# First chunk of a recurrent attention and expert kernel: transposed x made directly by matmuls, values loaded as fp32 and cast, state copied, a new order

## The chip, the cores and the metric

The kernel runs on one core of a Trainium2 chip. The metric is the device time of one execution in microseconds (us). A profiled execution gives a span from its first to its last instruction, which is shorter than the device time.

## The reference, cut to what matters

Two stages follow each other. The first is a gated recurrence over 768 steps for 4 batches and 8 heads of width 48; the second a mixture of 4 dense experts, each applied to every row.

```python
f = 1 / (1 + exp(-f_logit))
for t in range(768):
    state = f[:, :, t, :, None] * state + einsum('bhd,bhe->bhde', k[:, :, t], v[:, :, t])
    y[:, :, t] = einsum('bhd,bhde->bhe', q[:, :, t], state)
x = y.transpose(0, 2, 1, 3).reshape(3072, 384)
p = domain_probs / (domain_probs.sum(-1, keepdims=True) + 1e-9)
out = sum(p[:, e:e+1] * (relu(x @ w1[e]) @ w2[e]) for e in range(4))     # w1 384x1024, w2 1024x384
```

## The kernel before

**Tiling.** The sequence is cut into 6 chunks of 128 steps; in each chunk all 4 batches are worked on, so a chunk gives 512 rows of x. Inside a chunk the recurrence is turned into matmuls: cumulative sums of log gates (`cs`, `cq`), their exponentials (`exps`, `expq`), products of these with q and k (`q`, `k`), transposes of the products (`tpq`, `tpk`, evicted by `ev_tp`), scores (`at`, evicted through a causal mask by `ev_at0` and `ev_at1`; two of these go through ScalarE and a mask on GpSimd, `mask1`), and `y` = scores times values. Chunks behind the first add a product with the carried state. After `y`, `kv` makes the state's new part, `ev_kv` adds it to `Sf`, and GpSimd scales and casts it (`sf`).

**From y to the experts.** The experts need x transposed. In the first chunk, `ev_y` evicts y as bf16, `xt` transposes it by three TensorE transposes and `ev_xt` evicts that to the tile xT. Then the expert matmuls: `h` (w1 times xT, a unit being twelve 128-wide matmuls in chunk 0 and three 512-wide ones afterwards), `relu`, `o` (times w2). From the second half of chunk 1 on, other forms of these run (`hs` and `p`).

**Loads.** SyncE (SP) issues the loads of f, k and q, one per batch in chunk 0 (197 KB each; f and q in packets of 384 bytes, k in packets of 192). GpSimd (POOL) issues transfers that also cast: the values v of chunk 0 as bf16 (`vb`, line 284), and all weights (line 303), in eleven pieces w0 to w10: w0 and w1 are the two halves of expert 0's w1, w2 and w3 those of expert 1's w1, w4 and w5 those of expert 0's w2, w6 to w10 whole matrices. w0 to w3 are written in packets of 1,024 bytes (384 packets a piece), w4 and w5 in packets of 768 (512 a piece). POOL works in order, and also does elementwise work; a load that it issues may be held back by `GATE` until another transfer has landed. Before, POOL's order is v0, v1, v2, w0, v3, then w1 and so on. In later chunks v is loaded by SP as fp32 and cast by an engine. The last piece, w10, is issued when chunk 1's first k load has landed.

**Order.** Nothing is reordered at run time: each engine works through its own list. The list comes from a small planner (`Plan.run`, line 92): each step (`Op`) has a cost per engine, dependencies, buffers that it takes and frees, and a priority. The planner walks forward in time, and whenever an engine is free it starts the ready step with the smallest priority. Priorities are due times plus corrections from the table `MOVES`. All transfers share one planned engine, "DMA", which carries one transfer after the other. Where PE is planned to have a longer hole ahead of the first expert matmul, filler matmuls (line 1022) are put in.

Of the kernel before, what the change touches and what calls it, by code (L numbers as in the profile page):

```python
# [8 lines left out]
FP32 = mybir.dt.float32  # L9
# [5 lines left out]
MOVES = (  # L15
# [24 lines left out]
class Op:  # L40


    def __init__(self, name, costs, emit, prio, deps=(), takes=(), frees=(), lag=0.0):
        self.name, self.costs, self.emit, self.prio = name, costs, emit, prio
        self.deps = [d for d in deps if d is not None]
        self.takes, self.frees, self.lag = list(takes), list(frees), lag
        if name.split(" ")[-1].startswith("0.") and {"ACT", "DVE"} & set(costs):
            self.lag += 0.1
        self.end = self.start = self.engine = None
        self.pad = 0  # L50
        self.port, self.turn = False, None


class Plan:


    LATENCY = 0.2

    def __init__(self, rooms):
        self.moves = dict(m.split("=") for m in MOVES.split(";") if m)  # L60
# [3 lines left out]
    def add(self, *args, **kw):  # L64
        op = Op(*args, **kw)
        by, _, engine = self.moves.get(op.name, "0").partition("@")
        op.prio += float(by)
        if engine:
            op.costs = {engine: op.costs[engine]}
# [67 lines left out]
def kernel(  # L137
# [23 lines left out]
    NT = B * T  # L161
    N2 = NT // 2
# [18 lines left out]
    P.slot[SPARE] = P.rooms["ps_m"].pop()  # L181

# [35 lines left out]
    nc.vector.memset(Sf, 0.0)  # L218
# [14 lines left out]
    for nm, a in (("f", f_logit), ("q", q), ("k", k), ("v", v)):  # L233
# [12 lines left out]
        "mp": ([128, 512], FP32),  # L246
    }

    alias = {"xT": "x", "xs": "x", "hs": "h", "ys": "yb", "praw": "o"}
    inbank = ("hp", "op", "pp", "mp")  # L250

    def tl(kind, *key):
# [10 lines left out]
        return tiles[kind, key]  # L263

# [62 lines left out]
    def gate2(c, b, n):  # L327
        g = tl("gp", c, b // 2).rearrange("t b h d -> t (b h) d")
        if c == 0:
            nc.scalar.activation(out=g[:, hh(b), 0:D].rearrange("t (j h) d -> t h j d", j=2),  # L330
# [740 lines left out]
```

## Time and profile before

| what | value |
|---|---|
| device time, median of 3 runs (lowest, highest) | 288.47 us (287.62, 289.21) |
| profiled execution, span | 285.7 us |
| median less span | 2.8 us |
| TensorE (PE) busy | 277.4 us |
| first expert matmul (`h`, line 489) | 18.18 us |
| last instruction on a compute engine (DVE, line 607) begins | 282.41 us |
| mean granted TensorE clock | 1.000 |

The profiled execution has its own span; what lies around it is not in the profile, so the difference to the median of the runs is kept as it is. A row of a timeline reads: start in us, length in us, engine, line, operation, what is written, what is read, shape, count, and in brackets the idle time before and what ended it. PEld is TensorE's weight load. A row of a DMA view reads: queue, packets, MB, and the time that the packets took as a share of 16 engines; packets overlap, so that share can be over 100%. Rows of the view by stretches give the stretch, its length, then the busy time of each engine with its number of instructions, the granted clock, the DMA share and GB/s.

### The profile page before, as it was taken

Reading aid. Unit: us, or ns where it says so; the run is one execution under the profiler, and the core shown is the slowest. Engines: PE = TensorE matmul, PEld = TensorE weight load, DVE = VectorE, ACT = ScalarE, POOL = GpSimd, SP = SyncE. Lnnn points to the kernel's source line nnn. Section 1 sums busy time; section 2 is a strip of 40 time slices with the busy share of each in tenths; the row PEclk is TensorE's granted clock in tenths of the full one; section 3 lists DMA queues with packets and bytes.
Section 4 is the critical chain, followed back from the end, with each engine's and each line's share of the span. In section 5 each row is a group of like instructions: output and inputs, shape, how many; then the busy total and the mean of one; then the engine's idle time right before and its main releaser. Section 6 shows DMA issues by size and latency. Waiting matters only on the chain.

```text
span 285.7 us, 7476 instructions
## 1 busy us (share of the span) xinstructions
PE 277.4 (97%) x3016; PEld 236.7 (83%) x3020; DVE 196.1 (69%) x402; ACT 180.6 (63%) x336; POOL 114.1 (40%) x186
## 2 busy tenths in 40 slices
PE   6889999999999999999999999999999999999995
PEld 4667555657877999999999998999899998999994
DVE  5794144697779896875888848886888730874374
ACT  6768756568657963586668766658638348836710
POOL 5999101528663760866036756343750000000000
PEclk9999999999999999999999999999999999999999
DMA  6999999999977999999879999989675210050003
GB/s 157 214 199 207 208 192 205 178 202 178 183 142 151 160 197 155 210 184 185 178 150 189 164 224 210 144 191 158 74 164 107 57 55 2 19 122 31 2 0 110
DMA packets 153687, 41.85 MB, mean 146 GB/s; under 512 B 144029, under 2 KB 152861, under 8 KB 153653
## 3 DMA queue, kind: packets, MB, share of 16 engines
q1 hardware_dynamic: 142404, 34.66, 65.0%
q0 software_dynamic: 11248, 6.72, 16.3%
q8 instruction: 23, 0.38, 0.6%
q14 instruction: 12, 0.09, 0.1%
HBM read 31.51 MB, written 4.72 MB: 127 GB/s over the span
## 4 chain that ended last, share of the span: by engine, by line
PE 78%; DMA 14%; POOL 5%; SPq 1%; issue 0%; DVE 0%; POOLq 0%
PE ps_m L521 33%; PE ps_m L580 29%; DMA w_sb<-in_moe_w_dram 10%; PE ps_m L504 6%; PE ps_m L489 4%; DMA k<-in_k_dram 4%; POOL w_sb L303 2%; PE ps_m L428 2%; PE ps_m L455 1%; POOL vb L284 1%; PE ps_m L451 1%; PE ps_m L338 1%; PE ps_m L461 1%; POOL AT L432 1%; SPq L290 1%
## 5 line engine op out<-in xcount | busy, mean ns | idle before, releaser
L521 PE MATMUL ps_m<-x,w_sb 128*128 128x256 bf16 x864 | 104.8, 273 | 0.0
L529 ACT ACTIVATE h<-ps_m 128x512 bf16<-128x512 f32 x111 | 66.2, 598 | 46.1 <-PE ps_m L521 38.8
L521 PEld LDWEIGHTS <-w_sb 128*128 128x128 bf16 x864 | 82.9, 98 | 9.4
L580 PEld LDWEIGHTS <-S 128*128 128x128 bf16 x576 | 48.7, 98 | 0.9
L607 DVE TENSOR_TENSOR o<-ps_m,o 128x192 f32<-128x192 f32 x91 | 31.3, 354 | 22.0 <-PE ps_m L580 21.0
L580 PEld LDWEIGHTS <-h 128*128 128x128 bf16 x432 | 36.2, 98 | 0.6
L504 PE MATMUL ps_m<-w_sb,h 128*128 128x384 bf16 x192 | 35.3, 326 | 0.4 <-DMA w_sb<-in_moe_w_dram 0.4
L489 PE MATMUL ps_m<-x,w_sb 128*128 128x128 bf16 (+2 forms) x260 | 34.5, 281 | 0.6 <-DMA w_sb<-in_moe_w_dram 0.4
L411 ACT ACTIVATE yb<-ps_m,pn 128x384 bf16<-128x384 f32 x54 | 28.1, 584 | 7.7 <-PE ps_m L455 6.4
L476 POOL TENSOR_TENSOR Sf<-Sf,egs 48x192 f32<-48x192 f32 x40 | 21.0, 526 | 27.1 <-DVE Sf L468 17.4
L444 DVE TENSOR_TENSOR AT<-ps_m,mask 128x512 bf16<-128x512 f32 x40 | 25.2, 683 | 8.6 <-PE ps_m L428 8.5
L500 ACT ACTIVATE h<-ps_m 128x512 bf16<-128x512 f32 (+1 forms) x42 | 22.5, 536 | 12.8 <-PE ps_m L489 11.8
L489 PEld LDWEIGHTS <-w_sb 128*128 128x128 bf16 x264 | 21.7, 98 | 9.5 <-DMA w_sb<-in_moe_w_dram 0.6
L544 DVE TENSOR_TENSOR S<-h 128x1024 bf16<-128x1024 bf16 x36 | 25.2, 713 | 6.1 <-ACT h L529 5.5
L580 PE MATMUL ps_m<-ts_sb,S 128*128 128x192 bf16 x288 | 29.2, 246 | 0.0
L580 PE MATMUL ps_m<-w_sb,S 128*128 128x192 bf16 x288 | 28.7, 246 | 0.0
L504 PEld LDWEIGHTS <-h 128*128 128x128 bf16 x192 | 18.3, 98 | 12.5 <-DMA w_sb<-in_moe_w_dram 0.9
L388 POOL TENSOR_TENSOR qk<-q,e 128x384 bf16<-128x384 f32 x19 | 22.7, 1205 | 14.5 <-ACT e L371 9.7
L580 PE MATMUL ps_m<-w_sb,h 128*128 128x192 bf16 x288 | 28.0, 246 | 0.0
L527 DVE TENSOR_SCALAR h<-ps_m 128x512 bf16<-128x512 f32 x33 | 22.4, 691 | 8.1 <-PE ps_m L521 7.5
L371 ACT ACTIVATE e<-ps_m 128x384 f32<-128x384 f32 x40 | 23.4, 704 | 5.8 <-PE ps_m L338 5.4
L388 POOL TENSOR_TENSOR qk<-k,e 128x384 bf16<-128x384 f32 x20 | 20.2, 1016 | 16.7 <-PE ps_m L580 7.4
(87 smaller groups left out, 317.5 us busy)
## 6 DMA issues: line engine op xcount, KB each, us to landing
out_dram<-o SPq DMA_DIRECT2D x23, 192.0 KB, 2.3
w_sb<-in_moe_w_dram POOLq DMA_DIRECT2D x5, 768.0 KB, 16.3
k<-in_k_dram SPq DMA_DIRECT2D x10, 384.0 KB, 5.6
q<-in_q_dram SPq DMA_DIRECT2D x10, 384.0 KB, 5.2
v<-in_v_dram SPq DMA_DIRECT2D x10, 384.0 KB, 5.4
f<-in_f_logit_dram SPq DMA_DIRECT2D x9, 384.0 KB, 4.6
w_sb<-in_moe_w_dram POOLq DMA_DIRECT2D x6, 384.0 KB, 8.6
f<-in_f_logit_dram SPq DMA_DIRECT2D x6, 192.0 KB, 3.7
```

What stands on the lines that cost most here:

```text
L371: nc.scalar.activation(out=o, in_=i, func=AF.Exp, scale=1.0 if j else -1.0)
L388: return engines[eng].tensor_tensor(out=tl("qk", c, b)[:, j, :, 0:D].rearrange("t (i r) d -> t i r d", r=2), in0=tl("qk"[j], c, b // 2)[:, ...
L411: nc.scalar.activation(out=ys, in_=y, func=AF.Copy, scale=pe)
L444: nc.vector.tensor_tensor(out=tl("AT", c, b)[:, r].rearrange("s i t -> s (i t)"), in0=tl("A", c, b, r).rearrange("s i t -> s (i t)"), in1= ...
L489: nc.tensor.matmul(out=hp(c, e, fc, n0, n1, nf)[:, f], lhsT=w1_sb[:, e, kk, (fc + f) * 128:(fc + f + 1) * 128], rhs=tl("xT", c)[:, kk, n0: ...
L500: nc.scalar.activation(out=dst, in_=src, func=AF.Relu)
L504: nc.tensor.matmul(out=tl("op", c, e, nt)[:, 0:Din], lhsT=tl("h", c, e, half_of(c, nt * T))[:, fc, nt * T:(nt + 1) * T], rhs=w2_sb[:, e, f ...
L521: nc.tensor.matmul(out=out_[:, f], lhsT=w1_sb[:, e, kk, (fc + f) * 128:(fc + f + 1) * 128], rhs=tl("xs", c, hf, p)[:, el, kk, :], start=(k ...
L529: nc.scalar.activation(out=dst, in_=tl("hp", c, hf, p, el, fc), func=AF.Relu)
L544: return nc.vector.tensor_tensor(out=o, in0=in0, in1=in1, op=op)
L580: nc.tensor.matmul(out=out_, lhsT=lhs[:, f, :], rhs=rhs[:, f, :], start=(first and el == 0 and f == 0), stop=(el == 1 and f == KH - 1), sk ...
L607: nc.vector.tensor_tensor(out=o, in0=src, in1=o, op=ALU.add)
```

## The change

1. **Transposed x directly (`pe_yt`, `yt`).** For all four batches of chunk 0, the values stand in a zero-padded tile `vp` (128 zeros, then for each head 48 values and 128 zeros). A 128-column window of that tile is the stationary operand and the scores of one head the moving one, so that the result is already x transposed: ten 128-wide matmuls per batch into one PSUM tile `yT`, evicted once to xT (`ev_xt`; in two parts for the last batch). `y`, `ev_y` and `xt` of chunk 0 go.
2. **Values as fp32.** v of chunk 0 is loaded by SP, as in later chunks, and cast into `vp` by an engine (`cast_v`): batch 1's on VectorE, batch 2's on ScalarE, batch 0's on POOL, batch 3's on VectorE. POOL's four loads of v go.
3. **State copied.** In chunk 0 `ev_kv` copies into `Sf` instead of adding (on ScalarE for three batches, on VectorE for one), and Sf's memset goes; four memsets of `vp` (128x768 words each) come.
4. **A new order.** `MOVES` gives way to `RANKS`, a whole list of priorities, one for each step; planned costs and delays are set anew; `GATE` now holds w0 until batch 0's f has landed and w1 until batch 1's v has landed.

What the built program then does in chunk 0, engine by engine (numbers are batches):

- SP: f2, f1, q2, k2, q1, f0, k1, f3, v1, q3, q0, k0, the probabilities, k3, v2, v0, v3 (before: f0, f1, k2, f2, k1, k0, q0, q1, q2, f3, k3, q3, the probabilities).
- POOL: product k2, w0, product q1, w1, w2, product q0, mask of batch 2, w3, mask of batch 1, w4, w5, cast of v0, w6, and on with states and weights.
- DVE: product q2, product k1, QK of batch 2, cast of v1, scores of 2, QK of 1, product k0, product q3, product k3, QK of 0, scores of 1 and 0.
- ACT: gates and exponentials, scores of batches 2 and 1, cast of v2, two copies of QK of batch 3, eviction of x of batch 2, state copies, then relu.
- PE: the chunk's matmuls, `yt` of batch 2, scores of 0, `kv` of 2, scores of 3, the first `h` (batch 2, w0), `yt` and `kv` of 1, `yt` and `kv` of 0, `h` of batch 1 with w1 and w0, `h` of batch 0 with w1, `yt` of 3, and on. Six filler matmuls stand in place of ten.

The core of the diff:

```diff
-    LATENCY = 0.2
+    LATENCY = 0.14
...
+    for c, b in DIRECT:
+        nc.vector.memset(tl("vp", c, b), 0.0)
...
     def load(c, nm, b, n):
-        if (c, nm) == (0, "v"):
-            ins[c, nm, b] = nc.gpsimd.dma_start(out=tl("vb", c, b), in_=srcs[nm][c, :, b * H:(b + n) * H, :])
-            if f"v{b}" in GATE:
-                after(ins[c, nm, b], ins[GATE[f"v{b}"]])
-            return
...
+    def v_pad(b):
+        return tl("vp", 0, b)[:, T:].rearrange("t (h x) -> t h x", x=VP)[:, :, 0:D]
+
     def cast_v(c, b, eng):
-        return copy(eng, tl("vb", c, b), tl("v", c, b // 2)[:, hh(b), :])
+        return copy(eng, v_pad(b) if (c, b) in DIRECT else tl("vb", c, b), tl("v", c, b // 2)[:, hh(b), :])
+
+    def pe_yt(b):
+        for kk in range(KD):
+            heads = [h for h in range(H) if h * D < (kk + 1) * 128 and (h + 1) * D > kk * 128]
+            for h in heads:
+                w0 = T + h * VP - (h * D - kk * 128)
+                nc.tensor.matmul(out=tl("yT", 0, b)[:, kk, :], lhsT=tl("vp", 0, b)[:, w0:w0 + 128], rhs=tl("AT", 0, b)[:, h % 2, h // 2, :],
+                                 start=(h == heads[0]), stop=(h == heads[-1]))
...
+            if c == 0:
+                copy(eng, Sf[rows, b], KV[rows, :, r, :])
+            else:
+                nc.vector.tensor_tensor(out=Sf[rows, b], in0=Sf[rows, b], in1=KV[rows, :, r, :], op=ALU.add)
...
-ORDER = "f0 k0 q0 f1 k1 q1 f2 f3 k2 q2 k3 q3"
-SEQ = "v0 v1 v2 w0 v3 w1"
+ORDER = "f0 k0 q0 f1 k1 q1 v0 f2 k2 q2 v1 f3 k3 q3 v2 v3"
...
-GATE = {"v0": (0, "k", 1), "v1": (0, "k", 2)}
+GATE = {"w0": (0, "f", 0), "w1": (0, "v", 1)}
```

More of the change, by code (lines that the diff above doesn't have):

```diff
@@ L54 @@
 class Plan:
-    LATENCY = 0.2
+    LATENCY = 0.14
     def __init__(self, rooms):
-        self.moves = dict(m.split("=") for m in MOVES.split(";") if m)
+        self.ranks = RANKS.split()
         self.ops, self.rooms = [], {r: list(range(n)) for r, n in rooms.items()}
@@ L65, in add @@
         op = Op(*args, **kw)
-        by, _, engine = self.moves.get(op.name, "0").partition("@")
-        op.prio += float(by)
-        if engine:
+        rank = self.ranks[len(self.ops)]
+        op.prio = int(rank.rstrip("ADP"))
+        if rank[-1] in "ADP":
+            engine = {"A": "ACT", "D": "DVE", "P": "POOL"}[rank[-1]]
             op.costs = {engine: op.costs[engine]}
@@ L615, in add_load @@
     def add_load(c, nm, b, n, prio, deps=(), cost=None):
-        op = P.add(f"ld {nm}{c}.{b}", {"DMA": cost or (1.05 if c else 0.8 if nm in PAIRED else 1.1) * n}, lambda e: load(c, nm, b, n), prio,
-                   deps=deps, takes=[(nm, c, b // 2)], lag=2.0)
+        op = P.add(f"ld {nm}{c}.{b}", {"DMA": cost or (0.87 if c else 0.72 if nm in PAIRED else 0.87) * n}, lambda e: load(c, nm, b, n), prio,
+                   deps=deps, takes=[(nm, c, b // 2)], lag=10.5 if (c, nm, b) == (1, "f", 0) else 4.7 if c == 1 else 2.5)
         for i in range(n):
@@ L636 @@
     wd, fifo = {}, []
-    for j, x in enumerate(SEQ.split() + [f"w{i}" for i in range(SEQ.count("w"), len(pieces))]):
-        i = int(x[1:])
-        if x[0] == "v":
-            issued.append(P.add(f"v issue {i}", {"POOL": 0.8}, lambda _, i=i: load(0, "v", i, 1), -600 + 2 * j,
-                                deps=issued[-1:] + gate(x), takes=[("vb", 0, i)], lag=1.2))
-            ld[0, "v", i] = P.add(f"ld v0.{i}", {"DMA": 1.1}, lambda _: None, VW[0] + j, deps=issued[-1:] + fifo[-1:], lag=2.0)
-            fifo.append(ld[0, "v", i])
-            continue
-        e, which, ks, cols = pieces[i]
+    for j, (e, which, ks, cols) in enumerate(pieces):
+        i, x = j, f"w{j}"
         if i == 7:
-            add_load(1, "f", 0, 1, -454.5, deps=wd[2, 1], cost=0.1)
+            add_load(1, "f", 0, 1, -454.5, deps=wd[2, 1], cost=0.85)
         if i == w_last:
@@ L728, in attention @@
             at, vb = AT_[b], VB[b]
-            eA = [P.add(f"ev_at{r} {c}.{b}", {"ACT": 0.6} if c == 0 and f"{b}.{r}" in BYPOOL.split() else {"DVE": 0.685}, one(ev_at, r), s(7) + 0.1 + 0.1 * r, deps=[at],
+            eA = [P.add(f"ev_at{r} {c}.{b}", {"ACT": 0.735} if c == 0 and f"{b}.{r}" in BYPOOL.split() else {"DVE": 0.685 if c else 0.73}, one(ev_at, r), s(7) + 0.1 + 0.1 * r, deps=[at],
                         takes=[("AT", c, b)], frees=[pt_("A", r)]) for r in range(2)]
@@ L732, in attention @@
                 if c == 0 and f"{b}.{r}" in BYPOOL.split():
-                    eA[r] = P.add(f"mask{r} {c}.{b}", {"POOL": 0.65}, on(mask_at, r), s(7) + 0.2 + 0.1 * r, deps=[eA[r]])
-            y = P.add(f"y {c}.{b}", {"PE": 0.4 if c else 0.28}, on(pe_y), s(11), deps=eA + [vb, kvdone.get((c - 1, b))],
+                    eA[r] = P.add(f"mask{r} {c}.{b}", {"POOL": 0.8}, on(mask_at, r), s(7) + 0.2 + 0.1 * r, deps=[eA[r]])
+            if (c, b) in DIRECT:
+                y = P.add(f"yt {c}.{b}", {"PE": 0.57}, lambda e, b=b: pe_yt(b), s(11), deps=eA + [vb],
+                          takes=[pt_("yT")], frees=[("QK", c, b), ("AT", c, b), ("x", "vp", c, b)], lag=0.2)
+                Y.append(y)
+                parts = [slice(0, KD)] if b < B - 1 else [slice(0, 2), slice(2, KD)]
+                xdone[c, b] = [
+                    P.add(f"ev_xt {c}.{b}", {"ACT": 0.49, "DVE": 0.55} if len(parts) == 1 else {"ACT": 0.38, "DVE": 0.42} if ks.start == 0 else {"ACT": 0.27, "DVE": 0.29},
+                          lambda e, b=b, ks=ks: copy(e, tl("xT", c)[:, ks, b * T:(b + 1) * T], tl("yT", c, b)[:, ks]),
+                          s(13) + 0.1, deps=[y], takes=[("x", "xT", c)], frees=[pt_("yT")]) for ks in parts]
+                X.append(xdone[c, b])
+                continue
+            y = P.add(f"y {c}.{b}", {"PE": 0.386 if c else 0.21}, on(pe_y), s(11), deps=eA + [vb, kvdone.get((c - 1, b))],
                       takes=[pt_("y")], frees=[("QK", c, b), ("AT", c, b), ("vb", c, b)], lag=0.2)
@@ L1029 @@
 BLOCKED = ()
+DIRECT = ((0, 0), (0, 1), (0, 2), (0, 3))
+GATES = ((0, 1), (1, 1), (2, 1), (3, 1))
 YP, RP = 17, 50
```

88 lines of the change are left out of this document (44 added, 44 removed), and 76 rows, old and new, of tables (MOVES, RANKS).

## The prediction, made before the changed kernel had run

> **What bounds the kernel now.** I read the page's first lines, then TensorE's busy time by stage, its waits, the chain of waits from its end backwards, and last the DMA queues of the opening, packet by packet.
>
> ```profile
> span 285.7 us, 7476 instructions
> PE 277.4 (97%) x3016; PEld 236.7 (83%) x3020; DVE 196.1 (69%) x402; ACT 180.6 (63%) x336; POOL 114.1 (40%) x186
> ```
> TensorE (PE) is busy 97% of the span, so the stages are what to look at. Busy time by stretch (length, then PE, weight loads, DVE, ACT, POOL, granted clock, DMA share, GB/s):
>
> ```profile
> 15.00:20.00 5.00, 4.19 (x73) 3.45 (x74) 4.46 (x11) 2.83 (x7) 4.98 (x7) 1.00 1.47 197
> 20.00:25.00 5.00, 5.00 (x98) 4.93 (x95) 3.57 (x13) 4.02 (x9) 4.85 (x10) 1.00 1.27 206
> 25.00:58.00 33.00, 32.79 (x199) 17.97 (x200) 14.02 (x24) 21.35 (x35) 9.04 (x16) 1.00 1.18 198
> 58.00:282.00 224.00, 223.63 (x2543) 202.41 (x2543) 163.79 (x333) 142.28 (x266) 84.25 (x130) 1.00 0.73 134
> ```
> From about 18 us on PE has no holes; before that it waits for the first chunk's attention. The first expert matmul, PE's waits between 18.2 and 282 us, and the chain around the last weight piece:
>
> ```profile
> 18.18 0.84 PE L489 MATMUL ps_m<-x,w_sb 128*128 128x128 bf16 x12 [0.41 <-DMA w_sb<-in_moe_w_dram]
> ...
> PE ps_m L489 <- DMA w_sb<-in_moe_w_dram: 0.4, 1, 0.4
> PE ps_m L504 <- DMA w_sb<-in_moe_w_dram: 0.4, 1, 0.4
> ...
> 48.32 10.26 DMA w_sb<-in_moe_w_dram
> ...
> 58.63 0.82 PE ps_m L504 x4
> ...
> 282.41 0.36 DVE o L607
> ```
> So the time is: first expert matmul at 18.2, then unbroken PE work to 282.4, then a tail of 3.3. Weights arrive just in time: PE waits 0.4 us for the first piece (w0) and 0.4 us for the last (w10). A change to the first chunk can therefore win only by starting the expert stream earlier, and loses whatever it starts it later.
>
> **What sets the opening** is the order in which transfers land. Rows of the hardware queue (q1, the SP loads) and the software queue (q0, the POOL weights): packets, MB, time of the packets as a share of 16 engines. The windows are, in order, 2.3 to 9.9 us, 9.8 to 10.4, 19 to 22, 24 to 26, 39 to 42 (both queues) and 47 to 49.9:
>
> ```profile
> q1 hardware_dynamic: 6384, 1.81, 102.4%
> ...
> q0 software_dynamic: 133, 0.01, 39.9%
> ...
> q0 software_dynamic: 625, 0.62, 123.7%
> ...
> q0 software_dynamic: 526, 0.39, 128.6%
> ...
> q0 software_dynamic: 561, 0.45, 93.6%
> q1 hardware_dynamic: 558, 0.11, 32.4%
> ...
> q1 hardware_dynamic: 3573, 0.68, 117.1%
> ```
> Alone, the hardware queue moves 1,232 packets a us (3573 in 2.9 us), and a chunk-0 load (197 KB) takes 0.82 us (1.81 MB in 7.6 us). Alone, the software queue moves 200 of w0 to w3's 1 KB packets a us (625, less 24 of 4 bytes, in 3 us), or 263 of the 768-byte ones. Together, from 39 to 42 us, each moved 187 a us: **one packet for one packet**, though the software queue's are four times as long. A load of 192-byte packets then runs at 187 instead of 1,232 a us, six to seven times slower. Three landings show it; the rows are the delays from issue to landing of chunk 0's third q load (issued at 6.9, alone; the row holds f3 too), of v0 (issued at 7.6) and of the first f load of chunk 1 (issued at 32.5, 192 KB beside a running weight stream):
>
> ```profile
> DMA to landing us min/median/max: 3.8/3.9/3.9
> ...
> DMA to landing us min/median/max: 5.3/5.3/5.3
> ...
> DMA to landing us min/median/max: 11.5/11.5/11.5
> ```
>
> **The change part by part.** Removed per batch of chunk 0 are the y matmuls, their eviction and the three transposes; added are ten 128-wide matmuls (yt) and one eviction. The rows for the terms: the first read of a landed f, then PE, ACT, POOL and DVE. For yt, the first expert group is the nearest row: 0.84/12 = 0.07 us a matmul with its end, 0.21/3 = 0.07 for a weight load that nothing holds up:
>
> ```profile
> 3.94 0.52 ACT L325 ACTIVATE f<-f 128x384 f32<-128x384 f32 x1 [1.85 <-DMA f<-in_f_logit_dram]
> 14.02 0.36 PE L455 MATMUL ps_m<-vb,AT 128*128 128x48 bf16 x8
> 20.51 0.33 PE L480 MATMUL ps_m<-ident,yb 128*128 128x128 bf16 x3
> 20.46 0.21 PEld L480 LDWEIGHTS <-yb 128*128 128x128 bf16 x3
> 19.12 0.41 PE L428 MATMUL ps_m<-QK 48*128 48x128 bf16 x8
> 14.23 0.33 PE L461 MATMUL ps_m<-vb,qk 128*128 128x96 bf16 x4
> 14.56 0.50 ACT L278 CAST yb<-ps_m 128x384 bf16<-128x384 f32 x1
> 16.21 0.47 ACT L278 COPY x<-ps_m 128x384 bf16<-128x384 bf16 x1
> 18.20 0.59 ACT L278 COPY QK<-ps_m 112x512 bf16<-112x512 bf16 x1 [1.14 <-DVE QK L279]
> 12.20 1.00 POOL L388 TENSOR_TENSOR qk<-k,e 128x384 bf16<-128x384 f32 x1
> 18.30 0.66 POOL L432 TENSOR_SCALAR_AFFINE_SELECT AT<-AT 128x512 bf16<-128x512 bf16 x1
> 52.88 1.20 POOL L388 TENSOR_TENSOR qk<-q,e 128x384 bf16<-128x384 f32 x1 [0.19 <-issue]
> 56.52 0.52 POOL L279 CAST vb<-v 128x384 bf16<-128x384 f32 x1
> 7.90 1.02 DVE L388 TENSOR_TENSOR qk<-k,e 128x384 bf16<-128x384 f32 x2 [2.92 <-ACT e L373]
> 3.18 0.70 DVE L218 MEMSET Sf<- 112x768 f32 x1
> ```
> *PE work.* Per batch 0.36 + 0.33 goes and 10 x 0.07 comes: even. But less of the first chunk is done when the expert stream starts. Before, three transpose groups (0.21 to 0.33 each), one score group (0.41), two y (0.36) and two kv stand behind the first expert matmul, 1.76 to 2.12 us without the kv; after, three yt (0.70) and three kv, 2.43 with the third kv (0.33): +0.3 to +0.7. I take +0.3, since matmuls overlap their neighbours' ends.
>
> *Chain per batch.* One eviction (0.50) and one transpose group (0.33) leave it, about 0.8 us, which counts only if they end last.
>
> *Memsets.* Four of 128x768 for the padded values come (4 x 0.70) and Sf's 0.70 goes: +2.1 us on DVE, hidden by its 2.92 us wait before the first product. State copies replace adds off the path: 0. The new order of the later chunks: 0, since PE is full there (223.63 of 224.00) and stays so as long as no wait appears; every us it loses would be paid in full.
>
> *Values.* This is the term that decides. Before, POOL issued v0 to v2 ahead of w0, so weights reached the engines when nearly all SP loads had moved. After, v loads stand on SP, at places 9, 15, 16 and 17 of 17, and POOL issues w0 behind one product only. Step by step:
>
> 1. The sixth load, f of batch 0, which w0 waits for, lands at 3.9 + 5 x 0.82 = 8.0 (3.94 is when ACT first reads an f before). The product (1.00) is done by then. From issue at 7.6 to its first packets, between 9.8 and 10.4, v0 took some 2.2 us, so w0's packets start at 10.2. By 9.9 us 1.81 MB = 9.2 loads have moved, so q3 is nearly through; q0 (512 packets), k0, k3, v2, v0, v3 (1,024 each) are not.
> 2. From 10.2 on every weight packet is paired with a load's packet. A 768-byte pair takes 1/187 us, 1.5 ns more than the 1/263 of that packet alone; for 1 KB packets I take 1/200 + 1.5 ns, 154 a us. w0, w1, w2 (1,152 packets) run to 10.2 + 7.5 = 17.7. q3's rest (0.4) and q0 (512/154 = 3.3) are through at 13.9 and, 0.9 us later as for the others (q2, the ninth, landed at 10.7), landed at 14.8.
> 3. POOL, in order: product q0 (1.2) to 16.1, mask (0.66) to 16.8, then w3, whose packets start 2.2 later, 19.0. In the gap of 1.3 us the loads run alone (1,600 packets).
> 4. So k0 gets 585 packets by 17.7 and its last 440 in the gap, k3 all 1,024, v2 136. Beside w3 (384, 2.5 us, to 21.5) and w4 (512, 2.7 us, to 24.2) v2's other 888 pass: **v2 lands at 25.1.** Beside w5 (to 26.9) v0 gets half; POOL cannot issue w6 before it has cast v0, so the loads then run alone: **v0 lands at 28.2**, v3 at 29.0.
> 5. ACT, in order: cast of v2 (0.5), two copies of QK (2 x 0.59), eviction of x (0.5), with handovers 2.5 us: first expert matmul at 27.6. It, one yt and one kv fill 1.4 us to 29.0; the next yt waits for v0: 28.2 + 0.52 + 0.3 = 29.0. From there PE is dense.
>
> Queued behind the waiting instructions: on POOL, behind the product that waits for q0, the mask for the first yt and weights w3 to w5; behind the cast of v0, w6 and all later weights. These delays cost nothing more: w6 to w9, 0.79 MB each at 0.62 MB in 3 us, take 3.8 us each from 31.0 on and end near 47; w10, issued after a load of chunk 1 and taking 10.26, ends near 62; PE, 9.4 us late, asks for it at 68. On DVE, behind k0's product, the score evictions of two batches.
>
> *PE restart.* After 13 us PE has almost nothing to do until 25. How a stopped PE restarts the trace shows only at the very start, where four 192-wide matmuls take 0.80 us, and later 0.49, both at granted clock 1.00:
>
> ```profile
> 5.07 0.80 PE L342 MATMUL ps_m<-gp,Up 128*128 128x192 bf16 x4 [0.80 <-ACT gp L330]
> ...
> 9.47 0.49 PE L353 MATMUL ps_m<-gp,Wp 128*128 128x192 bf16 x4
> ```
> Bounds: 0, or half speed for the 4.2 us from 5.07 to 9.25, a loss of 2.1. I take 1.0, as part of it falls into the wait for v0. The Trainium skill, "TensorE: Matmul & The Clock Gate", Part 1, says that one idle window of about 3.4 us halves the array's clock and that about 3.4 us of sustained work restores it; by it the loss would be 1.7 and the sum 0.7 more. The trace agrees with the halving (0.80 against 0.49), and no row here shows the idle window.
>
> **Sum**, against the profiled execution: first matmul +9.4 (27.6 - 18.2), work left over +0.3, w10's wait gone -0.4, restart +1.0: +10.3 us, 285.7 to 296.0. The median of the runs, 288.47, is 2.8 above the span; kept, that gives **298.8 us**, 3.6% slower.
>
> **The rivals.**
> *A, loads keep their place (not slower).* If a chunk-0 load were not slowed by weights, v2, the fourteenth, would land at 3.9 + 13 x 0.82 + 0.3 (the probabilities) = 14.9, first matmul 2.5 later, 17.4: -0.8, +0.3, -0.4 gives 287.6, or a us better, 286.6, if the shorter chain brings as much on top. For it: the loads alone fill the engines (102.4%) from 2.3 us on, so most of them have moved when the weights start; it decides if the weights' first packets come after about 14 us. Against it: 561 to 558. The Trainium skill, "DMA: Bandwidth & Descriptors", "Issuing engine by pattern", puts simple loads on the Sync queue as generally faster, which favours this rival; 5.3 against 3.8 us agrees, the 11.5 us beside weights does not. The same page, "Queues, rings and completion order", has each engine go round the queues packet by packet, which for 1 KB packets no row here shows by itself. 0.15.
> *B, POOL's own wait saves the loads (slower, but mildly).* If q0 lands a us later (15.9), w3 starts at 20.1 and the gap, 2.4 us, moves 2,950 packets: v2 lands at 20.8 and the first matmul comes at 23.3; but v0 and v3 still go beside w3 to w5 and land at 25.3 and 29.2, so the yt of batch 0 costs a wait to 26.1 and that of batch 3, 4.2 us of work behind the first matmul, one to 29.9. That is as if the stream had begun at 25.7: +7.5, -0.1, restart 0.5, 296.4. Point 3 sits close to this. 0.14.
> *C, no gap (slower still).* If q3 and q0 get through before w0's packets, w3 follows w2 at once, 2,560 weight packets run to 25.7, v2 lands at 27.0 and the first matmul comes at 29.5: +11.3, -0.1, restart up to 2.1, 302. 0.11.
>
> **How the numbers follow.** Mine 0.60, B 0.14, C 0.11, A 0.15. About 0.5% (1.4 us) is what a measurement of this kernel can tell from no change. Slower: 0.60 + 0.14 + 0.11 = 0.85. A lies around that bound: faster 0.08, same 0.07. My own case spans about 296.5 to 300.5 (landing of q0 by 0.5 us either way, restart 0 to 2.1); with C above, and below an us or two for a B with a still longer gap, 294 to 302.5 leaves out A and the tails.
>
> **What would show it.** In the changed kernel's trace: delays from issue to landing of over 8 us for chunk 0's last k and v loads, where the q loads take under 4; equal packet counts of both queues between 11 and 17 us; ACT's cast of v2 and POOL's cast of v0 ended by a DMA; a first expert matmul between 23 and 30 us, PE idle ahead of it, and the same dense 224 us behind. It is wrong if those loads land by 16 us, or if PE shows new holes after 60 us.

## The result, and the profile after

The changed kernel takes 302.21 us (median of 4 runs, 300.24 to 305.27), the kernel before beside it 288.28 (287.62 to 289.21): ratio 1.0465, 95% interval 1.0403 to 1.0527. One disturbed run of the four is left out of the ratio. The profiled execution took 300.71 us, its span is 299.0; spans differ by 13.3 us, medians by 13.9.

The page's first lines, then PE by stretch in the columns used before the change (length, PE, weight loads, DVE, ACT, POOL, granted clock, DMA share, GB/s):

```profile
span 299.0 us, 7480 instructions
PE 282.3 (94%) x3012; PEld 241.0 (81%) x3012; DVE 211.4 (71%) x422; ACT 164.6 (55%) x314; POOL 114.0 (38%) x186
```
```profile
15.00:20.00 5.00, 1.85 (x16) 1.36 (x16) 1.46 (x2) 0.34 (x1) 4.73 (x6) 0.74 1.22 196
20.00:25.00 5.00, 0.61 (x4) 0.34 (x4) 1.79 (x3) 0.38 (x1) 0.06 (x1) 0.50 1.24 206
25.00:30.00 5.00, 4.81 (x51) 4.08 (x52) 1.34 (x2) 2.81 (x7) 0.00 (x0) 0.50 1.08 158
...
75.00:298.00 223.00, 219.29 (x2488) 199.35 (x2486) 171.45 (x345) 122.51 (x234) 82.25 (x128) 1.00 0.68 127
```
From 15 to 25 PE worked 9.19 us before and works 2.46 now, while the DMA engines move as much as ever (196 to 206 GB/s). The time is lost there. (PE's busy time grows as well, by 4.9 us; for one thing matmuls are slower at a granted clock of 0.50, the first expert group taking 1.46 us where it took 0.84. The last row reaches 2.6 us beyond PE's last matmul, which ends at 295.4.) What PE waits for, and its first expert matmul (`h`, line 536 here), on the timeline:

```profile
21.80 0.61 PE L441 MATMUL ps_m<-ident,qk 128*128 128x128 bf16 x4 [3.52 <-DVE qk L421]
25.19 1.25 PE L436 MATMUL ps_m<-AT,x 128*128 128x128 bf16 x10 [2.79 <-ACT x L316]
27.89 1.46 PE L536 MATMUL ps_m<-x,w_sb 128*128 128x128 bf16 x12
31.55 2.17 PE L536 MATMUL ps_m<-x,w_sb 128*128 128x128 bf16 x36
```
The first expert matmul comes at 27.89 instead of 18.18. The brackets name engines, and one step further back stands a transfer each time. ACT's cast of v2 and POOL's of v0, and the delay from issue to landing of the three v loads issued behind 11 us (v2, v0, v3):

```profile
24.62 0.51 ACT L316 CAST x<-v 128x384 bf16<-128x384 f32 x1 [9.28 <-DMA v<-in_v_dram]
...
30.11 0.50 POOL L317 CAST x<-v 128x384 bf16<-128x384 f32 x1 [10.05 <-DMA v<-in_v_dram]
...
DMA to landing us min/median/max: 13.1/13.6/15.1
```
Packets of the hardware queue (q1) and the software queue (q0) in three windows: 13.7 to 15.2, 15.5 to 20 and 25 to 28.5 us:

```profile
q1 hardware_dynamic: 1409, 0.34, 102.2%
q0 software_dynamic: 62, 0.05, 19.4%
...
q0 software_dynamic: 715, 0.71, 93.2%
q1 hardware_dynamic: 758, 0.14, 28.5%
...
q0 software_dynamic: 688, 0.52, 93.7%
q1 hardware_dynamic: 685, 0.13, 33.7%
```
In the two windows in which weights run, the loads get as many packets as the weights, 168 a us beside 1 KB packets and 196 beside 768-byte ones; where weights pause, 939 a us. The counts aren't equal everywhere: from 21.5 to 24.5 the loads got 439 and the weights 531; why, no row shows. Behind the first chunk PE has three new waits, 1.5 us together, all of them behind 60 us; before it had one of 0.4, for w10, which is gone. The last instruction on a compute engine:

```profile
PE ps_m L371 <- ACT gp L366: 0.8, 1, 0.8
PE ps_m L472 <- DVE QK L317: 0.5, 1, 0.5
PE ps_m L568 <- DMA x<-yb: 0.2, 1, 0.2
...
295.40 0.36 DVE L654 TENSOR_TENSOR o<-ps_m,o 128x192 f32<-128x192 f32 x1 [0.30 <-PE ps_m L627]
```

### The profile page after: what moved, and what is told of

It reads as the page before. It is cut to its first block, busy times and chain, and to the rows that moved or that the text cites. A ratio compares the mean times of both kernels' runs of the same rounds, so it can differ in the third digit from the quotient of the medians.

```text
span 299.0 us, 7480 instructions
## 1 busy us (share of the span) xinstructions
PE 282.3 (94%) x3012; PEld 241.0 (81%) x3012; DVE 211.4 (71%) x422; ACT 164.6 (55%) x314; POOL 114.0 (38%) x186
## 4 chain that ended last, share of the span: by engine, by line
PE 86%; DMA 8%; SPq 4%; DVE 1%; issue 0%; ACT 0%
PE ps_m L568 30%; PE ps_m L627 26%; PE ps_m L536 11%; PE ps_m L551 10%; DMA v<-in_v_dram 4%; SPq L323 2%; PE ps_m L472 2%; DMA f<-in_f_logit_dram 2%; DMA x<-yb 1%; PE ps_m L499 1%; PE ps_m L436 1%; PE ps_m L505 1%; SPq L325 1%; PE ps_m L495 1%; PE ps_m L371 1%; DVE S L591 1%
## 5 line engine op out<-in xcount | busy, mean ns | idle before, releaser
L576 ACT ACTIVATE h<-ps_m 128x512 bf16<-128x512 f32 x100 | 59.0, 597 | 61.2 <-PE ps_m L568 53.3
L654 DVE TENSOR_TENSOR o<-ps_m,o 128x192 f32<-128x192 f32 x91 | 31.0, 353 | 15.9 <-PE ps_m L627 11.2
L574 DVE TENSOR_SCALAR h<-ps_m 128x512 bf16<-128x512 f32 x44 | 29.9, 689 | 13.6 <-PE ps_m L568 13.1
L536 PE MATMUL ps_m<-x,w_sb 128*128 128x128 bf16 (+2 forms) x264 | 35.3, 286 | 0.0
L421 POOL TENSOR_TENSOR qk<-q,e 128x384 bf16<-128x384 f32 x19 | 23.6, 1246 | 14.2 <-DVE S L591 6.0
L547 ACT ACTIVATE h<-ps_m 128x512 bf16<-128x512 f32 (+1 forms) x39 | 19.3, 510 | 17.5 <-PE ps_m L536 10.9
L591 DVE TENSOR_TENSOR S<-h 128x1024 bf16<-128x1024 bf16 x36 | 26.0, 733 | 2.6 <-ACT h L576 1.8
L523 POOL TENSOR_TENSOR Sf<-Sf,egs 48x192 f32<-48x192 f32 x40 | 22.7, 571 | 8.2 <-ACT Sf L316 3.6
L455 ACT ACTIVATE yb<-ps_m,pn 128x384 bf16<-128x384 f32 x46 | 25.1, 583 | 1.3 <-PE ps_m L499 0.9
```

Source lines behind the costliest of these rows:

```text
L421: return engines[eng].tensor_tensor(out=tl("qk", c, b)[:, j, :, 0:D].rearrange("t (i r) d -> t i r d", r=2), in0=tl("qk"[j], c, b // 2)[:, ...
L455: nc.scalar.activation(out=ys, in_=y, func=AF.Copy, scale=pe)
L536: nc.tensor.matmul(out=hp(c, e, fc, n0, n1, nf)[:, f], lhsT=w1_sb[:, e, kk, (fc + f) * 128:(fc + f + 1) * 128], rhs=tl("xT", c)[:, kk, n0: ...
L574: nc.vector.tensor_relu(out=dst, in_=tl("hp", c, hf, p, el, fc))
L576: nc.scalar.activation(out=dst, in_=tl("hp", c, hf, p, el, fc), func=AF.Relu)
L591: return nc.vector.tensor_tensor(out=o, in0=in0, in1=in1, op=op)
```

## The experiments

The theory (starved loads): the values' loads, moved to SP's queue, meet the weights of POOL's queue and get one packet for each of theirs; the rest of the change costs little. Its rivals: yt or the new order is late by itself, or the values are slow through SP whatever the weights do.

**1. The first part alone (yt).** Into the kernel before go `pe_yt`, the padded tiles, their memsets and the one eviction; POOL casts the values straight into the padded tiles.

```diff
-            ins[c, nm, b] = nc.gpsimd.dma_start(out=tl("vb", c, b), in_=...)
+            ins[c, nm, b] = nc.gpsimd.dma_start(out=v_pad(b), in_=...)
...
+            if (c, b) in DIRECT:
+                y = P.add(f"yt {c}.{b}", {"PE": 0.65}, lambda e, b=b: pe_yt(b), ...)
```


> The kernel before with only the first part of the change: yt with padded values for chunk 0, one eviction to xT; y, its eviction and the three transposes of chunk 0 go. POOL goes on loading the values with a cast, now straight into the padded tiles; SP's and POOL's orders, the weights, the state's sum and all later chunks stay as before. Mine: the part costs about nothing: 0.8 us less of chain, +0.3 us of work behind the first expert matmul, in all 287.3 to 289.3. Rival, yt is dear by itself (2,048 more columns of moving data, four memsets on DVE): above 290. Rival, it is a gain that the other parts hide: below 287.

Measured: 288.03 us, ratio 0.9989 (0.9951 to 1.0028), span 285.9.

```profile
18.72 0.84 PE L506 MATMUL ps_m<-x,w_sb 128*128 128x128 bf16 x12 [0.86 <-DMA w_sb<-in_moe_w_dram]
```
PE is ready for it at 17.9 (18.72 less 0.86), before at 17.8, and w0 is what lands last in both. The 0.8 us of shorter chain don't show; yt is neither gain nor loss.

**2. The second part alone (values through SP), in before's own order.**

```diff
+            ins[c, nm, b] = nc.sync.dma_start(out=v32(b), in_=srcs[nm][c, :, b * H:(b + n) * H, :])
...
     def pe_y(c, b):
+        if c == 0:
+            copy(("DVE", "ACT", "DVE", "DVE")[b], tl("vb", 0, b), v32(b))
...
+        if i == 0:
+            after(ins["w", i], ins[0, "k", 0])
```


> The kernel before with only the second part of the change, in before's own order: SP issues v of chunk 0 as fp32 at the places at which the planner counted them (v0 twelfth, v1, v2 and v3 behind it), and an engine casts each right ahead of its y; POOL's four loads of v go, so w0 moves up, held until the sixth load (k0) has landed. All else, later chunks too, stays in place. Starved loads (mine): weights meet the loads from about 10.4 on with no pause; v0 has 2,000 packets ahead of it and lands near 24, the first expert matmul (batch 0) comes at 25 to 29, v1 to v3 land behind 33; device time 300 to 315. Rival, the values cost only their casts and the landing of the last loads: first expert matmul within 2 us of 18.2, 287 to 291.

Measured: 301.42 us, ratio 1.0450 (1.0374 to 1.0526), span 301.3: **a loss as large as that of the whole change comes with this part alone.** PE's waits for the casts, and the queues from 26 to 30 us:

```profile
PE ps_m L462 <- DVE vb L279: 10.1, 3, 3.9
...
q0 software_dynamic: 644, 0.65, 95.6%
q1 hardware_dynamic: 645, 0.12, 27.7%
```
The packets are 644 to 645. The first expert matmul came earlier than I had expected (21.8, not 25 to 29), because POOL paused between w0 and w1. Of the 10.1 us, 2.9 are a wait for v0's cast ahead of the first expert matmul, and 7.3 are two waits behind it, for v2 and v3. So the loss takes another way than in the changed kernel, where the first expert matmul is 9.7 us later and 1.5 us of waits follow: the cause is the same, but that the two sums are so alike is partly chance.

**3. The same, the weights held back.** One word: w0, and with it every weight, waits for the eleventh load instead of the sixth.

```diff
-            after(ins["w", i], ins[0, "k", 0])
+            after(ins["w", i], ins[0, "k", 3])
```


> As the run with the values alone in before's order, but w0, and with it every weight, is held until the eleventh load (k3) has landed, about 12.1, instead of the sixth. Starved loads (mine): by the weights' first packets, 14.4, 14 of 16 loads are through; v0 to v2 land by 15.5, only v3 goes beside weights (to about 24, which its y meets with a wait of 0 to 1.5 us); w0 lands near 18, first expert matmul at 18.5 to 20, device time 288.5 to 292. Rival, values through SP are slow whatever the weights do: within 3 us of the run that holds w0 until the sixth load.

Measured: 291.59 us, ratio 1.0101 (1.0039 to 1.0163), span 289.7. The delays of the v loads issued behind 11.2 us, POOL's issue of w0, PE's longest wait, the first expert matmul and PE behind it:

```profile
DMA to landing us min/median/max: 3.4/4.1/7.7
...
12.97 0.92 POOL L308 DMA_DIRECT2D w_sb<-in_moe_w_dram  x1 [8.05 <-DMA k<-in_k_dram]
...
PE ps_m L402 <- POOL qk L393: 1.1, 1, 1.1
...
19.46 1.46 PE L496 MATMUL ps_m<-x,w_sb 128*128 128x128 bf16 x12
...
28.25 3.44 PE L496 MATMUL ps_m<-x,w_sb 128*128 128x128 bf16 x33
...
20.00:25.00 5.00, 4.69 (x54) 4.23 (x53) 3.08 (x8) 1.84 (x4) 4.91 (x8) 0.50 1.24 205
```
Ten microseconds hang on the moment at which the weights start. That the values are slow through SP whatever the weights do, is out. Left against before are 3.7 us by the medians, 2.9 by the ratio: the first expert matmul comes 1.3 us later, and PE behind it runs at half clock. It doesn't wait for w0. The hold itself has a price: POOL works in order, so all that stands behind w0 in its list stood still for 8.05 us, and PE waits 1.1 us for the product that comes next on POOL, at 13.92.

**4. The same with fillers.** Nine filler matmuls in PE's short waits ahead of the first expert matmul.

```diff
+    for o in done:
+        o.pad = {'tpk 0.2': 4, 'at 0.2': 2, 'y 0.1': 3}.get(o.name, o.pad)
```


> The run with the values through SP in before's order and the weights held until k3 has landed (291.6; there the first expert matmul at 19.5 runs at half speed and PE loses 3.5 us between 19.5 and 30, against 0.7 in the kernel before), with nine filler matmuls of 512 columns in PE's short waits ahead of it: four ahead of k2's transposes, two ahead of the scores of batch 2, three ahead of the y of batch 1. Restart (mine): the clock is kept, the first group takes 0.84 instead of 1.46 us, and as the later chunks keep before's order, nothing takes the gain back: 2 to 3 us less, 288.6 to 289.8, so that the values through SP, timed rightly, cost 0.7 to 1.9 us against before. Rival, the clock falls for another reason or the gain is given back later as it was with the fillers in the changed kernel's order: 291 to 292.

Measured: 290.90 us, ratio 1.0102 (1.0072 to 1.0131), span 288.1.

```profile
19.22 0.84 PE L496 MATMUL ps_m<-x,w_sb 128*128 128x128 bf16 x12
21.33 0.37 PE L462 MATMUL ps_m<-vb,AT 128*128 128x48 bf16 x8 [0.76 <-DVE vb L279]
23.81 0.37 PE L462 MATMUL ps_m<-vb,AT 128*128 128x48 bf16 x8 [0.43 <-DVE vb L279]
26.37 3.45 PE L496 MATMUL ps_m<-x,w_sb 128*128 128x128 bf16 x33
```
A miss: the clock is kept, as expected, but the median falls by 0.7 us only, and the intervals overlap. The two profiles say where the rest went. From the first expert matmul to the group of 33 it took 8.79 us without fillers, 0.31 of it a wait for a v, and takes 7.15 with them, 1.19 of it such waits: half clock cost 2.5 us, and 0.9 of that comes back as waiting for values. The spans differ by 1.6.

**5. The changed kernel, weights behind the products.**

```diff
+    behind("w issue 0", "q 0.0")
+    behind("mask1 0.2", "w issue 0")
+    behind("w issue 1", "mask1 0.2")
+    behind("w issue 2", "w issue 1")
```


> The changed kernel with one thing moved: POOL issues w0 only behind the product of q0, and w1 and w2 behind the mask of batch 2 (w0 stood behind the product of k2, w1 and w2 behind that of q1). Nothing else moves. Starved loads (mine): the loads run alone until about 15.6 (q0 read at about 12.2, product 1.2, then 2.2 to the first packets), by when 16 loads at 0.82 us each from 2.3 on are through. v2 lands by 16.5 instead of 24.6, v0 and v3 by 17.5 instead of 30 and 31; w0 lands near 18.5, and the first expert matmul comes at 18.4 to 19.5 instead of 27.9. Device time 289 to 292. Rival, the new order and yt themselves are late (long chains on ACT and POOL): the loads move forward, but the first expert matmul stays behind 24, and the time above 296.

Measured: 295.55 us, ratio 1.0169 (1.0066 to 1.0271), span 294.6.

```profile
DMA to landing us min/median/max: 3.8/4.0/7.1
...
20.78 1.46 PE L536 MATMUL ps_m<-x,w_sb 128*128 128x128 bf16 x12 [2.26 <-DMA w_sb<-in_moe_w_dram]
28.30 3.47 PE L536 MATMUL ps_m<-x,w_sb 128*128 128x128 bf16 x42
```
The loads land as expected (4.0 instead of 13.6 us), and the first expert matmul is 7.1 us earlier. But it now waits for w0, PE runs at half clock behind it (0.50 from 20 to 25), and 6.7 of the 13.9 us come back, fewer than I had expected: the time lies between the two forecasts. Part of what is left is the price of holding the weights; whether there is also a loss that the values did not make, the seventh experiment asks.

**6. The same with fillers**, nine ahead of that first expert matmul (`o.pad = 9` for `h 0.0.0.256`).

> The changed kernel with POOL's weights behind the products (as in the first experiment), where the first expert matmul waits 2.3 us for w0 and is then run at half speed (1.46 against 0.84 us, granted clock 0.50 from 20 to 25), and with nine filler matmuls of 512 columns ahead of that matmul, 2.0 us at full speed, in the wait. Restart (mine): the fillers keep PE's clock, the first expert group takes 0.84 us, and the 2.7 us that the cold run lost between 20.8 and 30 against the run with values on POOL are back: 292 to 294 against 295.5. Rival, the matmuls are slow there for another reason (operands that transfers are writing): no change, 295 to 297.

Measured: 296.74 us, ratio 1.0276 (1.0208 to 1.0345), span 296.7. The two groups, PE's longest wait and the transfer behind it:

```profile
20.96 0.83 PE L536 MATMUL ps_m<-x,w_sb 128*128 128x128 bf16 x12
25.65 3.47 PE L536 MATMUL ps_m<-x,w_sb 128*128 128x128 bf16 x42
...
PE ps_m L371 <- ACT gp L366: 4.0, 2, 3.4
...
53.29 9.57 DMA f<-in_f_logit_dram
```
A miss in the time, but from the first expert matmul on PE is at full clock (granted 1.00 from 20 to 25, behind 0.66 from 15 to 20, so the fillers brought it back rather than kept it), and the group of 42 comes 4.69 us behind that matmul instead of 7.52. What is won by 26 us is lost again at 61, where PE waits 3.4 us for the gates of chunk 2, and the clock falls once more (0.80 from 58 to 75): their f load, issued at 53.3 beside w10, took 9.57 us (the changed kernel issued it at 61.7, and it took 4.5). So here the earlier start ran into one of the next loads.

**7. The changed kernel, values back on POOL.** All parts but the second: POOL issues v1, v2, v0, w0, v3, casting into the padded tiles; the engines' casts go.

```diff
+        if (c, nm) == (0, "v"):
+            ins[c, nm, b] = nc.gpsimd.dma_start(out=v_pad(b), in_=srcs[nm][c, :, b * H:(b + n) * H, :])
+            return
```


> The changed kernel with only the second part undone: POOL issues v of chunk 0 with a cast to bf16, written straight into the padded tiles, in the order v1, v2, v0, w0, v3, behind the product of k2; the four casts by engines go. yt, the copied state and the new order stay. Starved loads (mine): the weights now stand behind three value transfers in their own queue, so they reach the engines after about 15; SP's loads share with 192-byte packets only until then. First expert matmul at 18 to 19.5, device time 289 to 292, as the other parts cost +0.3 and at most 1.0. Rival, yt and the new order lose the time: above 296. Rival, the values were no loss but the others a gain: below 287.

Measured: 295.20 us, ratio 1.0209 (1.0135 to 1.0284), span 293.9.

```profile
20.83 0.84 PE L541 MATMUL ps_m<-x,w_sb 128*128 128x128 bf16 x12
22.97 2.17 PE L541 MATMUL ps_m<-x,w_sb 128*128 128x128 bf16 x36
...
PE ps_m L374 <- ACT gp L369: 2.3, 2, 1.6
```
My 289 to 292 is missed, and the rival's 296 nearly reached: 6 to 7 us (6.0 by the ratio, 6.6 by the medians) are lost without the values. Against the first part alone, which shares the values on POOL and yt, the first expert matmul is 2.1 us later, and PE waits 4.0 us behind it, longest for the gates of later chunks; the spans differ by 8.0, so 1.9 stand in no row shown. What differs is the new order (with the copied state, which runs off PE), and I had put it at nothing.

Part of the 2.1 us is a slow PE and not a late transfer. From 13.6 us to the first expert matmul PE has no hole, but until 20.2 its matmuls run slowly. The first yt here, PE's stretch around it, and the first yt of the first part alone:

```profile
18.46 1.27 PE L441 MATMUL ps_m<-AT,x 128*128 128x128 bf16 x10
...
15.00:20.00 5.00, 5.00 (x50) 4.03 (x48) 3.49 (x5) 3.08 (x7) 4.97 (x7) 1.00 1.46 197
...
13.98 0.72 PE L409 MATMUL ps_m<-AT,x 128*128 128x128 bf16 x10
```
The new order has six fillers in the opening where the kernel before has ten; that this is why PE is slow there is not shown. Nor does a run separate the order by itself from its fit: it was planned for values through SP, and here they come from POOL.

**8. One load of that order moved up.** PE waits 1.6 us at 134 for an f load of chunk 4.

```diff
+    behind("ld f4.0", "ld q3.0")
```


> The run of the changed kernel with values on POOL (span 293.9) with one move: in SP's list the first f load of chunk 4, issued at 129.0 and landed at 133.5, ahead of which PE then waits 1.6 us for its gates, goes eight places up, behind the first q load of chunk 3 (issued at 114.9). Late place (mine): in the new order this load stands too far back on SP's list; with it landed by 122, that wait goes, and with it a wait or two around it: 1.3 to 2.5 us less, span 291.4 to 292.6. Rival, the transfers are simply full there and the wait moves on to the next load: span 293.5 to 294.5.

Measured: 295.81 us, ratio 1.0208 (1.0134 to 1.0281), span 294.3.

```profile
127.18 0.84 ACT L361 ACTIVATE f<-f 128x768 f32<-128x768 f32 x1 [4.58 <-DMA f<-in_f_logit_dram]
...
PE ps_m L632 <- ACT h L581: 3.0, 1, 3.0
```
The rival was right: that wait went, and the next f load on the list, now later, held ACT for 4.58 us and PE with it for 3.0. (The move was six places, not the eight of the expectation.) This one place on the list isn't the cause; how the order as a whole makes up 6 to 7 us stays open.

**9. Smaller weight packets.** w0 and w1 of the changed kernel in halves of 256 columns.

```diff
+        if i < 2:
+            for j in range(2):
+                cs = slice(cols.start + j * F // 4, cols.start + (j + 1) * F // 4)
+                ins["w", i] = nc.gpsimd.dma_start(out=w[:, e, ks, cs], in_=r[e][:, ks, cs])
```


> The changed kernel with w0 and w1 each issued as two transfers of 256 columns, so that they are written in 512-byte packets, 1,536 in all instead of 768 of 1,024 bytes; the bytes are the same. Starved loads by packets (mine): beside these two pieces the loads get 1,536 packets instead of 768 at the cost of some 1.1 us; v2 lands 3 to 4 us earlier (21 to 22 instead of 24.6), the first expert matmul at 24 to 25.5, device time 2 to 4 us less than the changed kernel, 297 to 300. Rival, the queues share by bytes: v2 moves by less than 0.7 us or lands later, and the time stays within 1 us of the changed kernel or above it.

Measured: 302.36 us, ratio 1.0447 (1.0376 to 1.0518), span 300.5. The queues from 17 to 18 us (512-byte packets) and from 20 to 22 (1 KB), and the first expert matmul:

```profile
q0 software_dynamic: 265, 0.13, 96.3%
q1 hardware_dynamic: 228, 0.04, 39.0%
...
q0 software_dynamic: 316, 0.31, 90.8%
q1 hardware_dynamic: 318, 0.06, 27.7%
...
29.55 1.14 PE L543 MATMUL ps_m<-x,w_sb 128*128 128x128 bf16 x10
```
The time doesn't move and v2 landed at 26.3 instead of 24.6, so by these signs the rival holds. The rows speak against its reason: beside 512-byte packets the loads do get more, 228 a us against 159, so bytes are not what is shared. But POOL's list moved as well: the product of q0 no longer waited long, w3 was issued at 15.15 instead of 17.14, and the second pause in which the loads ran alone went (from 20 to 21 us they got 1,056 packets to the weights' 43 in the changed kernel; here, from 20 to 25, 856 to 854). The experiment changed two things, and is no clean test of the gain.

**10. Values alone, planned anew.** The first try at the second part alone gave the planner the four casts as steps of their own.

```diff
+            vb = P.add(f"v {c}.{b}", {"POOL": 0.52, "ACT": 0.53, "DVE": 0.45} if c == 0 else ...)
...
-GATE = {"v0": (0, "k", 1), "v1": (0, "k", 2)}
+GATE = {"w0": (0, "k", 0)}
```


> The kernel before with only the second part of the change: v of chunk 0 loaded by SP as fp32 behind the other loads and cast into vb by an engine; w0 held until the sixth SP load (k0) has landed, as in the changed kernel the sixth (f0). y, its eviction and the transposes stay. In this order POOL issues w0, w1 and w2 in one row. Starved loads (mine): weights meet the loads from about 10 on and never pause until POOL waits for q3; of the 6,400 packets left, v0 stands behind 3,300 and so lands behind 28, the first expert matmul comes behind 30, device time 300 to 310. Rival, the loads keep their place and the values cost only a cast: first expert matmul within 2 us of 18.2, device time 287 to 291.

Measured: 331.71 us, ratio 1.1461 (1.1388 to 1.1535), span 330.2; first expert matmul at 41.4. It starves as expected and more, but the planner also made another order of all later chunks, and PE waits there too. It mixes two causes; the second experiment replaces it.

**11. Fillers in the changed kernel itself**, eight ahead of k3's transposes and twelve ahead of the first yt.

> The changed kernel with filler matmuls of 512 columns in PE's two waits ahead of the first expert matmul: eight ahead of k3's transposes (the wait of 3.5 us) and twelve ahead of the first yt (the wait of 2.8 us). Restart, mostly hidden (mine): with the clock kept, the first expert group takes 0.84 instead of 1.46 us and begins 1 us earlier, but the yt of batch 0 still waits for v0 (landed at 30.0, cast by 30.6); only what runs cold behind 30.6 is won, 0.3 to 1.0 us of the span of 299.0, device time 299 to 302 by the runs' scatter. Rival, the restart is paid in full: 2.5 to 3 us less, span 296 to 296.5.

Measured: 300.47 us, ratio 1.0377 (1.0306 to 1.0447). That is 2.5 us under the changed kernel by the ratios and 1.7 by the medians, where I had given 0.3 to 1.0 and the rival 2.5 to 3; the intervals overlap, and the spans of the four executions, 296.1 to 301.5, cover both forecasts. Inconclusive: how much of the restart v0 hides stays open.

**12. The first part alone with w0 one place up**, the version that the first experiment points to.

```diff
+    behind("w issue 0", "v issue 1")
```


> The kernel before with the first part alone (span 285.9, where the first expert matmul at 18.7 waits 0.86 us for w0) and with w0 one place up on POOL, ahead of v2. Mine: w0 lands about 1 us earlier, v2 about 2 us later, which its yt at 19.8 does not meet; first expert matmul at 17.9, 0.5 to 0.9 us less than the first part alone, 287.0 to 287.6. Rival, the later loads take it back, or v2 comes too late: 288 to 289.

Measured: 287.96 us, ratio 1.0017 (0.9972 to 1.0061), span 286.0. w0 is no longer waited for; a transpose group ahead of the first expert matmul, at 17.79, now waits 0.53 us for a product, which itself waited 1.21 us for its q load, landing beside the transfers of POOL. The first expert matmul comes at 18.88, not earlier than 18.72. No version tried beats the kernel before.

## Why the prediction was right, and where it was not

| kernel | first expert matmul | ratio to before (95%) |
|---|---|---|
| yt alone | 18.72 | 0.9989 (0.9951 to 1.0028) |
| values through SP alone | 21.80 | 1.0450 (1.0374 to 1.0526) |
| the same, weights held back | 19.46 | 1.0101 (1.0039 to 1.0163) |
| all but the values | 20.83 | 1.0209 (1.0135 to 1.0284) |
| the whole change | 27.89 | 1.0465 (1.0403 to 1.0527) |

The mechanism is shown: the second part alone makes a loss of this size, and holding the weights back takes most of it away, there and in the changed kernel. Point by point, with the prediction's figure first:

- *Pair rates.* 154 a us beside 1 KB packets; 159 by the weights' count (715 in 4.5 us). 187 beside 768-byte ones; 196.
- *Points 1 and 2.* q0 was to land at 14.8; POOL's product of it began at 15.26. "w0, w1, w2 run to 17.7" failed: POOL's product of q1, which first waited 0.56 us, ended at 10.95 and held w1 up, so the weights paused from 13.7 to 15.2. I had listed that product and given it no time. I had also left out the gate of w1: v1 landed at 10.7, so without the product w1 would have been held for nearly as long. The pause let 1,409 packets of the loads through, and pushed all later weights back.

```profile
9.96 0.99 POOL L418 TENSOR_TENSOR qk<-q,e 128x384 bf16<-128x384 f32 x1 [0.56 <-ACT gp L363]
11.02 1.58 POOL L336 DMA_DIRECT2D w_sb<-in_moe_w_dram  x2
15.26 0.99 POOL L418 TENSOR_TENSOR qk<-q,e 128x384 bf16<-128x384 f32 x1 [2.66 <-DMA q<-in_q_dram]
```
- *Points 3 and 4.* The pause ahead of w3 had its size, 1,558 packets from 20 to 21.5 (1,600 from 17.7 to 19.0). v2 landed at 24.6 (25.1). That it came so close is partly luck: the first pause, which I had not seen, gave the loads packets early and pushed the second one back. The weights pushed back stood beside v0, whose cast began at 30.1 (landing 28.2).
- *Point 5.* First expert matmul 27.89 (27.6): v2 was 0.5 us early, and the chain from it took 3.3 us instead of 2.5. ACT's chain, on which I had counted, ended 2.4 us behind the landing (26.95); last came PE, which has two score groups and a kv ahead of that matmul and ran them, and yt, at half clock. The yt of batch 0 came at 30.67 (29.0).
- *Restart.* 1.0, bounds 0 and 2.1. From the first expert matmul to the group of 36 it took 3.66 us (27.89 to 31.55), and 2.14 with the values on POOL, where PE ran warm (20.83 to 22.97): 1.5. Where nothing else bound PE in that stage it was 2.8 (fifth and sixth experiment) and 2.5 (third and fourth).
- *w10's wait.* Gone, as predicted.
- *Signs.* The last k and the v loads behind it took 10.1 to 15.1 us to land, as said; k0 took 6.7, less than 8. Equal counts from 11 to 17 us hold only outside the pause. And one sign that I had named for being wrong came: PE shows new holes after 60 us.
- *Later chunks' new order: 0.* Mis-sized: it was put at nothing because PE was full there, and it brought 1.5 us of new waits in the changed kernel. With the values on POOL its price is larger, 6 to 7 us, and most of that doesn't add to the values' loss: 4.5% and 2.1% come to 4.65% and not to 6.6%. The whole change starts its experts 7 us later than the kernel without the values, and the sixth experiment shows one load that an earlier start has to wait for; that this holds for the rest is argued, not shown.

In sum, against the profiled executions: first expert matmul 9.7 (9.4), restart 1.5 (1.0), later waits 1.5 (0), w10 -0.4 (-0.4), work left over not measured by itself (0.3): 12.6 with that 0.3, where the last instruction came 13.0 later (295.40 less 282.41). The time was predicted 3.4 us below the median: the terms that were too small are the restart, by 0.5, the order's waits, by 1.5, and the first expert matmul, by 0.3. Of the other 1.1, 0.4 stands in no row shown, 0.3 behind the last instruction (3.6 us instead of 3.3), and 0.4 is the median's distance from the span, 3.2 instead of the 2.8 that I had kept.

The rivals: in A the loads keep their place; 168 packets a us speak against it. B needed a pause of 2.4 us ahead of w3; it was 1.5. C, no such pause, is close to what the ninth experiment ran into: it gave the first matmul at 29.5 and 302 us, and that kernel shows 29.55 and 302.36. So near an agreement is luck, as that kernel moves 3,328 weight packets in this stage and C counted 2,560.

## What to carry to other kernels

When a load moves from one queue to another, ask what runs beside it at that moment, and count packets, not bytes: here 192-byte packets got 168 a us beside 1 KB ones, and the loads 939 a us where those paused. Ahead of a critical load, a single wait that holds the bulk transfer back was worth ten microseconds in the kernel with the values alone; ask also what else stands in the list of the engine that does the waiting. And a static order has a due time built in: an earlier start in one stage is worth only as much as the loads of the next stages are early, as the one load of the sixth experiment shows.

## What was not expected of the hardware

- **PE's clock falls without a long wait.** With the values through SP and the weights held back, PE's longest wait between 14 us and the first expert matmul was 1.1 us, and yet the stretch from 20 to 25 shows a granted clock of 0.50 (the rows stand with the third experiment). The Trainium skill, "TensorE: Matmul & The Clock Gate", Part 1, has the halving follow one idle window of about 3.4 us; no wait of that length stands between 14 us and the first expert matmul in this trace. With fillers in the short waits, in the fourth experiment, every stretch reads 1.00; how much idling is enough, no run shows. Of the four runs of the third experiment's kernel the one with a mean clock of 0.998 had a span of 288.2, the others, at 0.986 to 0.987, 289.7 to 290.5, so the same program falls on either side.
- **The granted clock of a stretch doesn't tell all.** In the seventh experiment's kernel the stretch from 15 to 20 reads 1.00, and yet its yt takes 1.27 us, as long as in the fifth experiment at a granted clock of 0.50, where the first part alone shows 0.72. Beside that column, read the length of a matmul group whose full-speed length is known.
- **Three packet sizes, one rule.** Beside 512-, 768- and 1,024-byte packets the loads got 228, 196 and 159 packets a us (318 in 2 us), the software queue 265, 197 and 158. The Trainium skill, "DMA: Bandwidth & Descriptors", "Queues, rings and completion order", has each engine go round the queues packet by packet; the counts agree for the two longer sizes, and beside 512-byte packets the loads got 14% fewer than the weights.
